# Attention with beacon keys and a gated MLP on one core: first set's first values between the second and third scores, one MLP product before the fifth

## The chip, the cores and the metric

The kernel runs on one core of a Trainium2 chip. The metric is the device time of one execution in microseconds; the time quoted for a kernel is the median of its runs. The engines are named as in the profile: PE (TensorE, matmuls), PEld (its weight loads), DVE (VectorE), ACT (ScalarE), POOL (GpSimd) and SP (SyncE, which only issues transfers here).

## The reference

Two stages follow each other, and the result of the first is the input of the second. The first is causal attention for 8 batches of 8 heads, 576 queries of 64 elements, with 16 beacon keys and values put ahead of the ordinary ones. All queries may see the beacons.

```python
k_all = np.concatenate([beacon_k, k], axis=2)
v_all = np.concatenate([beacon_v, v], axis=2)
scores = scale * np.matmul(q, k_all.transpose(0, 1, 3, 2))
scores = np.where(causal, -1000000000.0, scores)      # beacons never masked
a = np.exp(scores - scores.max(-1, keepdims=True))
a /= a.sum(-1, keepdims=True) + 1e-09
attn = np.matmul(a, v_all)
x = attn.transpose(0, 2, 1, 3).reshape(B * S, H * D)  # 4608 tokens x 512
h = x @ w_in                                          # 512 x 2048
g = h * (1.0 / (1.0 + np.exp(-1.702 * h)))
out = g @ w_out                                       # 2048 x 512
```

## The kernel before, in words

**Sets.** A set is four heads of one batch, so there are 16 sets, two to a batch. A set's scores are computed transposed: keys lie on the partitions and queries along the free axis. The first four sets ("early") are handled in two halves of 288 queries. Only the parts on or below the causal diagonal are computed. A set's scores come in chunks of at most 512 columns for each of four heads, and each chunk goes into the one PSUM tile `s` (function `e_qk`, matmuls on L434). ScalarE takes its exponential into `E` (`e_exp`, L445), which frees `s` for the next chunk. Masks then cut the diagonal blocks: on VectorE for the first half of sets 0 and 1 (`e_mask`, L459, a minimum with a constant tile), on GpSimd otherwise (L466).

**Sums and values.** `e_av` (L521) multiplies `E` with ones, which gives the sums of the softmax, and with two halves of the values `vb`; that is three products for each half of a set. Their names here are sums, first values and second values. `e_z1` (L533) transposes the sums, `e_z2` takes the reciprocal (L540) and transposes it back (L544), and `e_norm` (L556) multiplies each value product by it into `xT`, the input of the MLP.

**MLP.** Tokens go in groups: two of 256, then of 512. `e_m1` (L580) is the product with `w_in`, one PSUM tile of 512 columns at a time. For the first two groups ScalarE takes a tanh (L594) and VectorE completes the gate (L613); later groups use a GELU on ScalarE (L601). The product with `w_out` is plain for the first two groups (L625), and for the others a scheme of seven half-size products (L694) with sums before (L645) and joins after (L710) on VectorE. `xT` is a ring of four batches, and the weights arrive in pieces during the opening.

**What sets the order.** The order of the work is written out by hand, a list of numbers for each engine in `ORDER`; a number is the place of an operation in the order in which the program creates them. `Plan.run` gives each operation a planned start, from constants for durations and latencies, and emits the operations by planned start; the order on each engine is that of its list. The planned times have one more use: all products but the scores share four PSUM tiles, and `Plan.run` gives a product the tile whose last reader ends first by plan. The semaphores that really hold an engine come from the data and the tiles, not from the planned times.

**Queues.** The opening's loads of queries, keys, values and weights are issued on GpSimd, whose list also holds masks. Such a load waits for the landing of the eighth load before it. The beacon keys are issued on SP after two memsets of VectorE, and the stores leave on SP.

The numbers that the change moves are these. On TensorE: 76, 100, 106, 108 and 111 are the first to fifth scores, namely the first half of set 0, the first half of set 1, and the three chunks of the second half of set 0; 129 are the sixth, of set 1. 115, 118 and 120 are sums, first and second values of the first half of set 0; 138, 141 and 143 the same of set 1. 155 and 152 are the second and the first product of the first MLP group. On VectorE: 78 is the last mask of the first half of set 0, and 105, 104 and 102 are the masks of the first half of set 1; 87 is a memset for beacon keys. 116 and 117 are `e_z1` and `e_z2` of set 0, 119 and 121 its normalising; 139, 140, 142 and 144 are those of set 1; 157 is a gate.

The softmax here doesn't subtract the row's maximum and nothing guards it: scores larger than these inputs give would overflow.

## Time and profile before

| What | Value |
|---|---|
| Runs | 329.97, 332.07, 331.99 us |
| Median | 331.99 us |
| Span of the profiled execution | 328.1 us |
| Profiled execution's own time | not given apart from its span |
| TensorE clock granted | 1.000 over the span |
| TensorE busy | 309.3 us, 94% |
| VectorE, ScalarE, GpSimd busy | 235.9, 202.0, 114.0 us |
| First score matmul | at 8.38 us |
| TensorE's idle stretches in the opening | 2.04 us to 11.47, 2.04 us to 14.54, 1.58 us to 20.01 |
| Bytes read and written in HBM | 37.22 and 9.44 MB |

The span is the time from the first to the last instruction of one profiled execution. A line of the view in order of time reads: start in us, time from start to end of the merged instructions, engine, line of the kernel, operation, tiles written and read, their form, and how many instructions were merged; in brackets stands how long the engine was idle before it and what ended that. Matmuls are pipelined and their ends are modelled, so neighbouring lines can overlap. A line of waits reads: engine and line that waited, what it waited for, the sum in us, how often, and the longest.

### The profile page before, as it was taken

Reading aid. Unit: us, or ns where it says so; the run is one execution under the profiler, and the core shown is the slowest. Engines: PE = TensorE matmul, PEld = TensorE weight load, DVE = VectorE, ACT = ScalarE, POOL = GpSimd, SP = SyncE. Lnnn points to the kernel's source line nnn. Section 1 sums busy time; section 2 is a strip of 40 time slices with the busy share of each in tenths; the row PEclk is TensorE's granted clock in tenths of the full one; section 3 lists DMA queues with packets and bytes.
Section 4 is the critical chain, followed back from the end, with each engine's and each line's share of the span. In section 5 each row is a group of like instructions: output and inputs, shape, how many; then the busy total and the mean of one; then the engine's idle time right before and its main releaser. Section 6 shows DMA issues by size and latency. Waiting matters only on the chain.

```text
span 328.1 us, 9811 instructions
## 1 busy us (share of the span) xinstructions
PE 309.3 (94%) x4288; PEld 210.0 (64%) x4288; DVE 235.9 (72%) x478; ACT 202.0 (62%) x236; POOL 114.0 (35%) x178
## 2 busy tenths in 40 slices
PE   0489999999999999999999999999999999999995
PEld 0367665544775467745878878547764776447884
DVE  3657788777987989977998798958557843006674
ACT  1567597687767686679767686868477212674010
POOL 8765487190319312951078019400042000000000
PEclk9999999999999999999999999999999999999999
DMA  7999999194424921693029809600120012000122
GB/s 126 161 202 209 203 187 181 34 99 103 113 67 72 186 50 34 70 191 57 2 45 177 133 2 122 157 0 2 37 96 2 2 34 78 18 0 2 65 98 97
DMA packets 58219, 28.81 MB, mean 88 GB/s; under 512 B 41280, under 2 KB 53568, under 8 KB 58176
## 3 DMA queue, kind: packets, MB, share of 16 engines
q0 software_dynamic: 47552, 18.49, 47.8%
q1 hardware_dynamic: 10560, 9.69, 9.1%
q8 instruction: 33, 0.54, 0.7%
q14 instruction: 10, 0.08, 0.1%
q10 hardware_dynamic: 64, 0.01, 0.0%
HBM read 37.22 MB, written 9.44 MB: 142 GB/s over the span
## 4 chain that ended last, share of the span: by engine, by line
PE 89%; ACT 4%; DVE 3%; DMA 2%; issue 1%; POOL 0%; DVEq 0%; ACTq 0%; POOLq 0%
PE u L580 36%; PE u L694 30%; PE s L434 9%; PE u L521 9%; PE u L625 4%; ACT E L445 3%; DMA qn<-in_q_dram 2%; DVE qT L405 1%; DVE sA L645 1%; DVE xT L556 1%; DVE rz L544 0%; DVE zt L533 0%; ACT L601 0%; DVE osb L710 0%; DVE rc L540 0%
## 5 line engine op out<-in xcount | busy, mean ns | idle before, releaser
L580 PE MATMUL u<-xT,w 128*128 128x512 f16 (+1 forms) x704 | 130.4, 340 | 0.5 <-ACT g L601 0.5
L445 ACT ACTIVATE E<-s 128x2048 f16<-128x2048 f32 (+5 forms) x66 | 98.9, 1515 | 46.0 <-PE s L434 45.6
L601 ACT ACTIVATE g<-u 128x512 f16<-128x512 f32 x128 | 70.5, 598 | 53.8 <-PE u L580 53.4
L580 PEld LDWEIGHTS <-w 128*128 128x128 f16 x704 | 67.8, 98 | 53.9 <-issue 1.5
L466 POOL TENSOR_SCALAR_AFFINE_SELECT E<-E 128x512 f16<-128x512 f16 (+3 forms) x78 | 49.3, 663 | 113.4 <-ACT E L445 81.6
L710 DVE SCALAR_TENSOR_TENSOR osb<-u,osb 128x512 f32<-128x512 f32 x56 | 37.2, 682 | 24.7 <-PE u L694 22.4
L694 PEld LDWEIGHTS <-g 128*128 128x128 f16 x512 | 48.4, 98 | 9.3 <-issue 0.2
L694 PE MATMUL u<-w,g 128*128 128x256 f16 x384 | 50.6, 273 | 0.0
L434 PE MATMUL s<-qT,kT 32*128 32x32 f16 (+20 forms) x1376 | 35.4, 232 | 14.4 <-DVE qT L405 8.4
L434 PEld LDWEIGHTS <-kT 32*128 32x128 f16 x1376 | 25.8, 94 | 30.6 <-issue 15.0
L694 PEld LDWEIGHTS <-sA 128*128 128x128 f16 x384 | 36.3, 98 | 5.3 <-issue 0.3
L694 PE MATMUL u<-tB,sA 128*128 128x256 f16 x256 | 35.0, 273 | 0.1
L645 DVE TENSOR_TENSOR sA<-g 128x512 f16<-128x512 f16 x32 | 12.9, 415 | 26.2 <-ACT g L601 26.2
L556 DVE TENSOR_TENSOR xT<-u,rz 128x352 f16<-128x352 f32 (+2 forms) x52 | 25.6, 517 | 6.9 <-PE u L521 6.7
L365 POOL DMA_DIRECT2D vb<-in_v_dram x32 | 27.4, 874 | 2.3 <-DMA kn<-in_k_dram 1.5
L521 PE MATMUL u<-E,vb 128*32 128x352 f16 (+8 forms) x928 | 28.0, 267 | 0.0
L484 DVE TENSOR_TENSOR zs<-zs,E 128x1344 f16<-128x1344 f16 (+2 forms) x36 | 22.7, 633 | 5.3 <-POOL E L466 4.4
L521 PEld LDWEIGHTS <-vb 128*32 128x32 f16 (+1 forms) x928 | 20.2, 99 | 5.9 <-issue 1.7
L405 DVE STREAM_TRANSPOSE kT<-kn 128x576 f32<-128x576 f32 x16 | 20.1, 1258 | 2.4 <-DMA kn<-in_k_dram 1.6
L405 DVE STREAM_TRANSPOSE qT<-qn 128x576 f32<-128x576 f32 x16 | 19.8, 1239 | 0.1
L533 DVE STREAM_TRANSPOSE zt<-u 128x224 f32<-128x224 f32 (+2 forms) x32 | 14.9, 471 | 6.6 <-PE u L521 6.5
L484 DVE TENSOR_TENSOR zs<-E 128x1856 f16<-128x1856 f16 x12 | 15.8, 1319 | 3.3 <-POOL E L466 3.3
(44 smaller groups left out, 237.7 us busy)
## 6 DMA issues: line engine op xcount, KB each, us to landing
out_dram<-osb SPq DMA_DIRECT2D x36, 256.0 KB, 2.5
kn<-in_k_dram POOLq DMA_DIRECT2D x16, 288.0 KB, 6.7
qn<-in_q_dram POOLq DMA_DIRECT2D x16, 288.0 KB, 6.6
vb<-in_v_dram POOLq DMA_DIRECT2D x24, 128.0 KB, 6.6
w<-in_moe_w_in_dram POOLq DMA_DIRECT2D x8, 256.0 KB, 9.9
w<-in_moe_w_out_dram POOLq DMA_DIRECT2D x4, 512.0 KB, 14.2
vb<-in_v_dram POOLq DMA_DIRECT2D x8, 112.0 KB, 5.0
vb<-in_v_dram POOLq DMA_DIRECT2D x8, 80.0 KB, 7.9
```

The costliest lines, as they stand in the source:

```text
L365: nc.gpsimd.dma_start(out=t[0 : hi - lo, j, h0:h1, :], in_=v[b, h0:h1, lo:hi, :].rearrange("h n d -> n h d"),)
L405: nc.vector.transpose(out=f32(dst.rearrange("p n e -> p (n e)")).rearrange("p (r t) -> p t r", t=TR), in_=f32(src[:, :]).rearrange("p (t c ...
L434: nc.tensor.matmul(sc[:, h, o : o + w], kT[s % NB2][r : r + 32, j * P : (j + 1) * P, d], qT[s % NB2][r : r + 32, a : a + w, d], start=(d = ...
L445: nc.scalar.activation(out=Es[s][:, :, c0:c1], in_=ss[i][:, :, o : o + c1 - c0], func=AFT.Exp, scale=0.125,)
L466: nc.gpsimd.affine_select(out=blk, in_=blk, compare_op=ALU.is_ge, fill=0.0, base=off + (Nb if j == 0 else 0), pattern=[[0, Q], [1, w]], ch ...
L484: nc.vector.tensor_tensor(out=t, in0=E[:, :, Z0:S] if i == 1 else t, in1=E[:, :, wcol[i] : wcol[i] + S - a], op=ALU.add,)
L521: nc.tensor.matmul(u[32 * h : 32 * h + 32, a:e], lhs, src[0:kw, h, col : col + e - a], start=first, stop=last,)
L556: nc.vector.tensor_tensor(out=xT[:, 2 * hs + x : 2 * hs + x + n, t0 : t0 + w], in0=rings[("av", s, x, half)][:, 0 : n * w].rearrange("p (n ...
L580: nc.tensor.matmul(u[:, o + a - t0 : o + e - t0], w1t[:, kp, nt * P : (nt + 1) * P], xT[:, kp, a % XR : (e - 1) % XR + 1], start=(kp == 0) ...
L601: nc.scalar.activation(out=gts[g][:, n0:n1, 0:w], in_=rings[("m1", g, n0)][:, 0 : n * w].rearrange("p (n w) -> p n w", n=n), func=AFT.Gelu ...
L694: nc.tensor.matmul(u[:, HM * mt : HM * (mt + 1)], lhs[:, n, mt * P : (mt + 1) * P], rhs[:, n, :], start=(n == 0 and mt == 0), stop=(n == H ...
L710: nc.vector.scalar_tensor_tensor(out=osbs[(g, dst)][:, :], in0=rings[("p", g, p)][:, :], scalar=scale_of(g), in1=osbs[(g, src)][:, :], op0 ...
```

## The change

Two lists are reordered in their first rows. On TensorE the three products of the first half of set 0 come directly after the second scores; they stood, mixed with those of set 1, after the third. The products of set 1 stay after the third scores, now alone. The second product of the first MLP group comes before the fifth scores and not after them. On VectorE `e_z1` of set 0 comes before the first mask of set 1, `e_z2` of set 0 before that set's last mask, and set 0's normalising before `e_z1` of set 1. The lists of ScalarE, GpSimd, SP and the loads are the same.

The other edits concern the planner alone. Its limit of eight loads in flight is applied in the order in which loads are issued, and no longer by dependencies set at creation. The cost of a change of TensorE's mode becomes a constant, and durations change in the plan for scores, products with `E`, masks on GpSimd, sums, transposes, the weights' sums and the GELU. No instruction takes these numbers, but planned times choose the PSUM tiles.

```diff
     "PE": [
-        76, 100, 106, 138, 115, 141, 118, 143, 120, 108, 111, 155, 152, 129, 161, 158, 122, 131, 164, 167, 134, 127,
+        76, 100, 115, 118, 120, 106, 138, 141, 143, 108, 155, 111, 152, 129, 161, 158, 122, 131, 164, 167, 134, 127,
...
     "DVE": [
-        73, 74, 75, 97, 98, 99, 80, 81, 82, 78, 105, 87, 104, 102, 139, 116, 117, 121, 119, 140, 144, 142, 157, 154,
+        73, 74, 75, 97, 98, 99, 80, 81, 82, 78, 116, 105, 87, 104, 117, 102, 121, 119, 139, 140, 144, 142, 157, 154,
...
+    LANES = 8
...
+                    if o.lands is not None and len(flight) >= self.LANES:
+                        if flight[-self.LANES].end is None:
+                            break
+                        t = max(t, flight[-self.LANES].end + self.LAT["Q"])
...
-                        if o.mode != mode:
-                            dur += 95 + 0.75 * tail / 2.4
-                        mode, tail = o.mode, o.tail
+                        m = o.mode
+                        if m != mode:
+                            dur += 114
+                        mode = m
...
+                    if o.lands is not None:
+                        flight.append(o.lands)
...
-        if len(flight) >= LANES:
-            deps = list(deps) + [flight[-LANES]]
         i = plan.op("POOL", dur, deps, emit, due=due, pr=pr, name=name)
-        flight.append(plan.op("Q", ns, [i], lambda: None, name=name + "q"))
-        return flight[-1]
+        i.lands = plan.op("Q", ns, [i], lambda: None, name=name + "q")
+        return i.lands
...
-        w = sum(max(45, 2 * x / 2.4 + 6) for x in ps)
+        w = sum(2 * x / 2.4 + 10.5 for x in ps)
...
-                    d = 50 + 4 * (e - a) / 1.92 if eng == "DVE" else 140 + 0.875 * 4 * (e - a)
+                    d = 50 + 4 * (e - a) / 1.92 if eng == "DVE" else 190 + 0.9 * 4 * (e - a)
...
-                op("DVE", 75 + 0.6 * 4 * w, deps + sums[-1:], lambda i=i: e_zadd(s, i), pr=3, name="zadd")
+                op("DVE", 70 + 0.56 * 4 * w, deps + sums[-1:], lambda i=i: e_zadd(s, i), pr=3, name="zadd")
...
-                "PE", sum(y / 2.4 + 6 for y in w), deps,
+                "PE", sum(y / 2.4 + 3.2 for y in w), deps,
...
-                    "DVE", 65 + 1.045 * cols, [avs[(s, x, half)], z2s.get(two_back(s, half))], lambda h=half: e_z1(s, h), pr=0, closes=key, name="z1"
+                    "DVE", 98 + 1.045 * cols, [avs[(s, x, half)], z2s.get(two_back(s, half))], lambda h=half: e_z1(s, h), pr=0, closes=key, name="z1"
...
-                    "DVE", 310 + 1.04 * cols, [z1] + [norms.get((*two_back(s, half), y)) for y in range(2)],
+                    "DVE", 340 + 1.04 * cols, [z1] + [norms.get((*two_back(s, half), y)) for y in range(2)],
...
-            prev = [op("DVE", 1550, w2_ld + (prev if i < 3 else [tds[0]]), lambda i=i: e_t(i, "DVE"), pr=3, due=TDUE, name="t")]
+            prev = [op("DVE", 1200, w2_ld + (prev if i < 3 else [tds[0]]), lambda i=i: e_t(i, "DVE"), pr=3, due=TDUE, name="t")]
...
-                    "ACT", 480, [pe], lambda n0=n0, n1=n1: e_gelu(g, n0, n1),
+                    "ACT", 490, [pe], lambda n0=n0, n1=n1: e_gelu(g, n0, n1),
```

More of the change, by code (lines that the diff above doesn't have):

```diff
@@ L112 @@
         "eng", "dur", "deps", "pr", "due", "emit", "kind", "ring", "mode", "lat",
-        "start", "end", "left", "users", "ready", "seq", "name", "tail", "table",
+        "start", "end", "left", "users", "ready", "seq", "name", "count", "table", "lands",
     )
 class Plan:
+    LANES = 8
     LAT = {"PE": 230, "ACT": 178, "DVE": 212, "POOL": 110, "Q": 1400, "SP": 0}
@@ L127, in __init__, with op @@
         self.closers = {}
-    def op(self, eng, dur, deps, emit, kind="", pr=5, due=0, ring=None, closes=None, mode=None, name="", tail=0, table=None):
+    def op(self, eng, dur, deps, emit, kind="", pr=5, due=0, ring=None, closes=None, mode=None, name="", count=0, table=None):
         o = Op()
         o.eng, o.dur, o.emit, o.kind, o.pr, o.due = eng, dur, emit, kind, pr, due
-        o.ring, o.mode, o.name, o.tail, o.table = ring, mode, name, tail, table
+        o.ring, o.mode, o.name, o.count, o.table = ring, mode, name, count, table
         o.deps = [d for d in deps if d is not None]
-        o.start = o.end = None
+        o.start = o.end = o.lands = None
         o.users = []
@@ L150, in run @@
         free.update(POOL=900, SP=700)
-        mode, tail, table, order = "m", 0, "e", []
+        mode, table, order = "m", "e", []
         bank = [None] * self.ring
+        flight = []
         while any(todo.values()):
@@ L728, in due_of @@
         return 0 if i < NCH0 else T_ATT0 + T_CH * (i - NCH0)
-    LANES = 8
-    flight = []
     def pool_load(dur, ns, deps, emit, due=0, pr=0, name=""):
-        if len(flight) >= LANES:
-            deps = list(deps) + [flight[-LANES]]
         i = plan.op("POOL", dur, deps, emit, due=due, pr=pr, name=name)
-        flight.append(plan.op("Q", ns, [i], lambda: None, name=name + "q"))
-        return flight[-1]
+        i.lands = plan.op("Q", ns, [i], lambda: None, name=name + "q")
+        return i.lands
     op = plan.op
@@ L804, in chunk @@
         ps = [x[0] for x in qk_pieces(i)]
-        w = sum(max(45, 2 * x / 2.4 + 6) for x in ps)
+        w = sum(2 * x / 2.4 + 10.5 for x in ps)
         qks[i] = op(
             "PE", w, deps, lambda: e_qk(i), kind="qk", pr=0,
-            due=0, mode="r", name=f"qk{i}", tail=ps[-1],
+            due=0, mode="r", name=f"qk{i}",
         )
@@ L867, in values @@
             avs[(s, x, half)] = op(
-                "PE", sum(y / 2.4 + 6 for y in w), deps,
+                "PE", sum(y / 2.4 + 3.2 for y in w), deps,
                 lambda x=x, half=half: e_av(s, x, half), kind="av",
                 pr=(16 * s + (n if whole else 8 * half)) if s >= HS else half,
-                ring=key, mode="c", name=f"av{s}.{x}.{half}", tail=w[-1],
+                ring=key, mode="c", name=f"av{s}.{x}.{half}",
             )
```

## The prediction

> **What bounds the kernel now.** I read the page's busy shares first, then the chain that ended last, then the waits of TensorE after the opening, and only then the opening itself, engine by engine, in order of time. The page:

> ```profile
> PE 309.3 (94%) x4288; PEld 210.0 (64%) x4288; DVE 235.9 (72%) x478; ACT 202.0 (62%) x236; POOL 114.0 (35%) x178
> DMA  7999999194424921693029809600120012000122
> PE 89%; ACT 4%; DVE 3%; DMA 2%; issue 1%; POOL 0%; DVEq 0%; ACTq 0%; POOLq 0%
> ```

> The first line says that TensorE is busy for 94% of the 328.1 us, the third that 89% of the last chain are matmuls. The DMA digits are slices of 8.2 us: the transfers run at nine tenths or more from 8 to 57 us. The waits of TensorE from 38 us to the end are one line:

> ```profile
> PE u L580 <- ACT g L601: 0.5, 1, 0.5
> ```

> So from 38 us on there is half a microsecond of waiting to win. What is loose lies in the opening. TensorE there, columns start, length, instruction, then idle time and what ended it:

> ```profile
> 11.47 1.04 PE L434 MATMUL s<-qT,kT 32*128 32x288 f16 x24 [2.04 <-ACT E L445]
> 14.54 0.83 PE L434 MATMUL s<-qT,kT 32*128 32x288 f16 x24 [2.04 <-ACT E L445]
> 15.30 1.05 PE L521 MATMUL u<-E,ones 128*32 128x288 f16 x24
> 16.16 1.80 PE L521 MATMUL u<-E,vb 128*32 128x288 f16 x48
> 17.90 0.54 PE L434 MATMUL s<-qT,kT 32*128 32x192 f16 x24
> 20.01 0.55 PE L434 MATMUL s<-qT,kT 32*128 32x208 f16 x32 [1.58 <-ACT E L445]
> 20.49 1.92 PE L580 MATMUL u<-xT,w 128*128 128x256 f16 x16
> 22.34 0.54 PE L434 MATMUL s<-qT,kT 32*128 32x288 f16 x24
> ```

> Second scores end at 12.5; TensorE is idle for 2.04 us until ScalarE has emptied the one score tile; third scores at 14.54; then all six products of sums and values of both sets, 2.6 us (15.38 to 17.97 in the chain), and only then the fourth scores, though their exponential was done at 16.89. After them 1.58 us more of idleness. From 20.0 to 66 us TensorE has no gap over 0.14 us. VectorE in the same stretch:

> ```profile
> 13.51 0.26 DVE L459 TENSOR_TENSOR E<-E,keep 128x192 f16<-128x192 f16 x1 [1.01 <-ACT E L445]
> 13.96 0.36 DVE L459 TENSOR_TENSOR E<-E,keep 128x512 f16<-128x512 f16 x1
> 14.53 0.39 DVE L459 TENSOR_TENSOR E<-E,keepb 128x448 f16<-128x448 f16 x1 [0.21 <-ACT E L445]
> 15.98 0.91 DVE L533 STREAM_TRANSPOSE zt<-u 128x288 f32<-128x288 f32 x2 [1.06 <-PE u L521]
> 19.52 0.82 DVE L556 TENSOR_TENSOR xT<-u,rz 128x288 f16<-128x288 f32 x2
> ```

> It waits 1.01 and 1.06 us, and ends the normalising of both sets at 20.34. The third view is GpSimd, whose queue carries load issues and masks alternately:

> ```profile
> 26.43 0.75 POOL L378 DMA_DIRECT2D w<-in_moe_w_out_dram  x1 [0.53 <-DMA w<-in_moe_w_in_dram]
> 29.21 0.54 POOL L354 DMA_DIRECT2D vb<-in_beacon_v_dram  x1 [1.33 <-DMA w<-in_moe_w_out_dram]
> 29.75 1.07 POOL L466 TENSOR_SCALAR_AFFINE_SELECT E<-E 128x512 f16<-128x512 f16 x2
> ```

> The load at 29.21 is held until an earlier transfer has landed, and the last masks of the second set stand behind it.

> [...] So I checked spacing rather than 94%: the 48 matmuls of 512 columns from 70.38 take 10.52 us, 219 ns each. [...]

> **The change, part by part.** Nothing is added or removed on the chip; two engines' orders change, and constants in the planner. I follow the clock of the trace, starting from events that don't move: second scores done at 12.55, the second set's exponentials at 13.47 and 14.49.

> *Set 0's sums and values moved ahead of the third scores.* Their last mask ends at 12.49, the last value block that they need landed at 12.46. Six products took 2.6 us, so one is 0.43. Sums 12.57 to 13.00, values to 13.87: wholly inside the 2.04 us of idleness, cost nothing. If a value block came late, the product would wait at the head of the queue and the third scores with it; they have 0.67 us of cover. The third scores stay at 14.54, since ScalarE sets them.

> *Set 0's transpose of sums (z1) ahead of the second set's first mask on VectorE.* z1 began 0.17 after its product, so 13.2, and takes 0.42 to the next start. The mask that ran at 13.51 starts at 13.65, the memset of the beacon keys at 13.9 instead of 13.77 (its key loads on SP land by 21.7 and are cast at 37), the second mask at 14.1. Then reciprocal and transpose of set 0 (0.25 + 0.40) before the third mask: 15.14 to 15.53 instead of 14.53 to 14.92. This is the added cost: everything queued behind waits, and set 1's sums on TensorE start at 15.60 instead of 15.30, an idle 0.2 us.

> *What TensorE then has.* Three products of set 1, 15.60 to 16.90. The fourth scores come as their exponential ends, 16.95 instead of 17.9: **1.0 us sooner**. Set 0's two normalisings run on VectorE from 15.45 to 16.3 under set 1's products. Set 1: z1 16.2, reciprocal 16.7, transpose to 17.4, two normalisings to 18.29 (20.34 before).

> *One MLP product ahead of the fifth scores.* It needs the last normalising, so it starts at 18.36 and ends at 19.29. Its weights landed at 15.67. The fourth exponential runs 17.53 to 18.98; the fifth scores could start at 19.0 and start at 19.29: 0.3 lost there, 0.93 of MLP work done in an idle stretch of 1.58. Fifth exponential 19.93 to 21.38, second MLP product to 20.76, sixth scores 21.44. Before, they followed the second MLP product at 22.41. **Gain at this point 0.95 us.** The next product needs weights that landed at 21.39 and starts at 21.9: 0.5 of cover left. On GpSimd the first set's mask follows its exponential from 20.04 to 19.05, and the third set's key load behind it from 20.46 to 19.5; the load after that stays at 21.68, held by the landing at 21.39, and so do the masks at 22.23 to 23.30, which TensorE wants only at 23.8.

> *Where part of it goes back.* With 0.95 the second set's last exponential ends at 28.7 instead of 29.68, but its masks stand behind the load held at 29.21. That load waits for a transfer in a full DMA, which nothing here brings forward. Masks still end at 30.82. The second set's second-half sums, on TensorE at 31.46 in the chain, would be due at 30.5; they wait to 30.9 (0.05 to 0.1 after the mask, as other releases show). **0.55 us is left.** The halves after it follow with it: scores of the third set 37.24 to about 36.7, for which keys landed at 33.23 and queries at 34.20, needed at 33.9 and 35.4.

> *Later.* Fixed landings have room (kn of the fifth set 47.73 for a use at 52.05; w_out rows by 42.6 for 45.0), so 0.55 goes to the end: span 328.1 to 327.55.

> *Planner constants.* They are not instructions, but planned times choose which of four PSUM tiles a product takes. By hand, the first deals exchange tiles among themselves with each free by 0.5 us or more. Later deals I have not worked out. Gain is bounded by the 0.5 us of waits after 38 us; cost is open: each bad deal holds TensorE for up to one reader, 0.68 us for a join, 0.60 for a GELU. I take zero and keep 0.5 below, 2.5 above for the range.

> **Against the runs.** The page has no time of the profiled run but its span; 331.99 lies 3.9 above it, the lowest run 1.9. I keep 3.9: 327.55 + 3.9 = 331.4. Three runs of one kernel spread over 2.1 us, or 0.6%; one per cent (3.3 us) is about what a measurement of this kernel can tell from no change.

> **Rivals.** *The whole 0.95 arrives* (chance 0.12): the held load goes out sooner because a transfer lands sooner. For: the third set's keys are issued one microsecond earlier. Against: they are queued behind, not ahead of, what it waits for. 331.0. *Nothing is left* (0.15): VectorE's longer queue, or weights at 21.39 landing half a microsecond later, eat the rest. For: covers of 0.5; against: both stay covered in my sum. 332.0. *Slower* (0.11): the deal of PSUM tiles. Place: the eight product groups after 70 us, where ScalarE, VectorE and TensorE share four tiles. One join's wait (0.68) per group is 5.4 us less 0.55: 336.9. It decides against "no change" from 3.3 + 0.55 = 3.9 us, six such waits. Against: the same rule, earliest tile to come free, gave next to none before. *The order does nothing* (0.03): would need TensorE not to take work in the stated order; 332. *Over 1% faster* (0.04): the three idle stretches of the opening sum to 5.66 us, but 2.04 of it lies ahead of every edit; the other 3.62 would have to vanish whole, or the runs' spread help; about 328.5.

> **The numbers.** Forecast 0.55, 331.4. Within 1%: 0.55 + 0.12 + 0.15 + 0.03 = 0.85. Faster 0.04, slower 0.11. The range goes from 331.0 less the 2.0 by which a run fell below the median, 329.0, to 331.4 plus the 2.5 kept for bad deals, 333.9.

> **What would show it.** Right: sums of set 0 on TensorE at 12.6; fourth scores at 16.9; an MLP product between fourth and fifth scores from 18.4; sixth scores at 21.4; masks of set 1 still at 29.75; TensorE idle 0.3 to 0.4 before the sums behind them; third set's scores at 36.7. Wrong: values waiting for a load near 13; the third mask after 15.6; masks leaving GpSimd before 29.5; and, above all, new waits of TensorE on ScalarE or VectorE after 38 us.

## The result, and the profile after

The changed kernel takes 329.24 us, the median of eight runs between 328.77 and 329.64; the kernel before takes 330.76 next to it, eight runs between 329.97 and 332.07. The ratio is 0.9946, with a 95% interval from 0.9922 to 0.9971. So the change is worth about half a per cent, 1.5 us, where I forecast 0.55 us. Most runs of the kernel before stand at 330.3, and three to five in ten of them (16 of 54 in one set of runs, 18 of 37 in another) in a second group, most of it around 332 us; the changed kernel has no second group. That is needed below, because the median of the kernel before moves with the share of that group.

The profiled execution of the changed kernel has a span of 327.8 us, against 328.1 before. On the page, span, busy shares, transfers and chain barely move:

```profile
span 327.8 us, 9812 instructions
PE 310.9 (95%) x4288; PEld 210.6 (64%) x4288; DVE 236.4 (72%) x478; ACT 202.0 (62%) x236; POOL 114.5 (35%) x178
DMA  7999999193424921692039809600120002000122
PE 89%; ACT 4%; DVE 3%; DMA 2%; SPq 1%; issue 0%; DVEq 0%; ACTq 0%
```

TensorE is busy for 1.6 us *more* with the same 4288 matmuls: the first hint, since nothing was added. From 38 us on its waits are the same single line as before:

```profile
PE u L589 <- ACT g L610: 0.5, 1, 0.5
```

The lines of the kernel are 9 higher than before from there on (L434 is L443, L521 is L530, L580 is L589). Now the opening on TensorE, in order of time:

```profile
11.88 1.04 PE L443 MATMUL s<-qT,kT 32*128 32x288 f16 x24 [2.15 <-DVE qT L414]
12.85 0.62 PE L530 MATMUL u<-E,ones 128*32 128x288 f16 x12
13.29 1.04 PE L530 MATMUL u<-E,vb 128*32 128x288 f16 x24
14.97 0.83 PE L443 MATMUL s<-qT,kT 32*128 32x288 f16 x24 [0.65 <-ACT E L454]
15.73 0.62 PE L530 MATMUL u<-E,ones 128*32 128x288 f16 x12
16.16 1.03 PE L530 MATMUL u<-E,vb 128*32 128x288 f16 x24
17.36 0.83 PE L443 MATMUL s<-qT,kT 32*128 32x192 f16 x24 [0.16 <-ACT E L454]
18.12 1.94 PE L589 MATMUL u<-xT,w 128*128 128x256 f16 x8
20.00 0.62 PE L443 MATMUL s<-qT,kT 32*128 32x208 f16 x32
20.55 1.05 PE L589 MATMUL u<-xT,w 128*128 128x256 f16 x8
22.21 0.54 PE L443 MATMUL s<-qT,kT 32*128 32x288 f16 x24 [0.62 <-ACT E L454]
```

Two things are to be seen. The idle stretches of 2.04 and 1.58 us ahead of the third and the fifth scores have become 0.65 and nothing. And the same work has two prices: the first MLP product, 8 matmuls of 256 columns, takes 1.94 us and the second 1.05. The trace's record of the granted clock (the rate at which TensorE is let run) tells why: it begins at 20.21 us with full rate. Until then TensorE ran at half that: the last five matmuls of the first product start 213 or 214 ns apart, those of the second, from its second on, 109 or 110. So the second idle stretch went in part because the product in it took twice as long; in a second trace, e4 below, with the clock up at 18.41, 0.31 us are left of it. (The views by window print full rate for a stretch that lies ahead of the first record; there the spacing of the matmuls is the evidence.) In the trace of the kernel before, the rise stood at 17.73 us, ahead of its MLP products. On VectorE:

```profile
13.52 0.48 DVE L542 STREAM_TRANSPOSE zt<-u 128x288 f32<-128x288 f32 x1 [0.73 <-PE u L530]
13.93 0.26 DVE L468 TENSOR_TENSOR E<-E,keep 128x192 f16<-128x192 f16 x1
15.30 0.35 DVE L468 TENSOR_TENSOR E<-E,keepb 128x448 f16<-128x448 f16 x1
17.75 0.82 DVE L565 TENSOR_TENSOR xT<-u,rz 128x288 f16<-128x288 f32 x2
```

The last line ends at 18.57, where it ended at 20.34 before, though this execution's third scores began 0.43 us later: its queries landed later.

What I passed over shows in the traces below. They hold half-rate stretches of 3.41 us (e9, from 21.52), 6.83 (e8, 13.43 to 20.26) and 10.24 (e5, 13.57 to 23.81), which are one, two and three times 3.41, and the rise lies at another place in each of seven traces of the kernel before, between 17.68 and 19.18 us.

### The profile page after: what moved, and what is told of

Same layout as the page of the kernel before. It is cut to its first block, busy times and chain, and to the rows that moved or that the text cites. A ratio compares the mean times of both kernels' runs of the same rounds, so it can differ in the third digit from the quotient of the medians.

```text
span 327.8 us, 9812 instructions
## 1 busy us (share of the span) xinstructions
PE 310.9 (95%) x4288; PEld 210.6 (64%) x4288; DVE 236.4 (72%) x478; ACT 202.0 (62%) x236; POOL 114.5 (35%) x178
## 4 chain that ended last, share of the span: by engine, by line
PE 89%; ACT 4%; DVE 3%; DMA 2%; SPq 1%; issue 0%; DVEq 0%; ACTq 0%
PE u L589 37%; PE u L703 30%; PE u L530 9%; PE s L443 9%; PE u L634 5%; ACT E L454 3%; DMA bkf<-in_beacon_k_dram 2%; DVE sA L654 1%; SPq L393 1%; ACT L610 0%; DVE kT L414 0%; DVE qT L414 0%; DVE rz L553 0%; DVE xT L565 0%; DVE zt L542 0%
## 5 line engine op out<-in xcount | busy, mean ns | idle before, releaser
L589 PE MATMUL u<-xT,w 128*128 128x512 f16 (+1 forms) x704 | 131.5, 342 | 0.5 <-ACT g L610 0.5
L589 PEld LDWEIGHTS <-w 128*128 128x128 f16 x704 | 68.0, 98 | 54.3 <-issue 1.7
L719 DVE SCALAR_TENSOR_TENSOR osb<-u,osb 128x512 f32<-128x512 f32 x56 | 37.2, 683 | 24.5 <-PE u L703 22.5
L443 PE MATMUL s<-qT,kT 32*128 32x32 f16 (+20 forms) x1376 | 35.8, 234 | 12.5 <-DVE qT L414 10.8
L443 PEld LDWEIGHTS <-kT 32*128 32x128 f16 x1376 | 26.1, 95 | 29.4 <-issue 13.6
L530 PE MATMUL u<-E,vb 128*32 128x352 f16 (+8 forms) x928 | 28.2, 268 | 0.0
L530 PEld LDWEIGHTS <-vb 128*32 128x32 f16 (+1 forms) x928 | 20.2, 98 | 5.9 <-issue 1.7
```

The source lines that it names most:

```text
L443: nc.tensor.matmul(sc[:, h, o : o + w], kT[s % NB2][r : r + 32, j * P : (j + 1) * P, d], qT[s % NB2][r : r + 32, a : a + w, d], start=(d = ...
L530: nc.tensor.matmul(u[32 * h : 32 * h + 32, a:e], lhs, src[0:kw, h, col : col + e - a], start=first, stop=last,)
L589: nc.tensor.matmul(u[:, o + a - t0 : o + e - t0], w1t[:, kp, nt * P : (nt + 1) * P], xT[:, kp, a % XR : (e - 1) % XR + 1], start=(kp == 0) ...
L719: nc.vector.scalar_tensor_tensor(out=osbs[(g, dst)][:, :], in0=rings[("p", g, p)][:, :], scalar=scale_of(g), in1=osbs[(g, src)][:, :], op0 ...
```

## The experiments

Two theories stood against each other at first. **A:** the order is worth what its waits give, and on top of it TensorE's half clock in the opening costs the two orders different amounts. **B:** the clock rises where the program puts it and has no part in the gain. A third, **C**, was the rival of the prediction: the planner's constants and the deal of PSUM tiles.

To compare traces in spite of different landings of the first loads, I use the time from the start of the third scores, which ScalarE sets in both orders, to the end of the span. In the table, "rise" is the last time in the opening at which the clock goes to full.

| Trace | Rise, us | Third to sixth scores | Third scores to end |
|---|---|---|---|
| before | 17.73 | 7.80 | 313.54 |
| before, six more traces | 17.68 to 19.18 | 7.60 to 8.17 | 313.35 to 313.93 |
| after | 20.21 | 7.24 | 312.85 |
| after again (e4) | 18.41 | 6.92 | 312.52 |
| order only (e2) | 21.41 | 7.42 | 313.02 |
| sets only (e11) | 24.42 | 9.07 | 314.81 |
| MLP product only (e12) | 24.96 | 9.20 | 315.28 |

### The kernel before and the changed kernel once more; order and constants apart

e1 and e4 are the two kernels unchanged. e2 takes the two lists of the change and leaves the planner as it was; e3 the reverse.

```diff
 e2, against before: only the first rows of "PE" and "DVE" in ORDER
-        76, 100, 106, 138, 115, 141, 118, 143, 120, 108, 111, 155, 152,
+        76, 100, 115, 118, 120, 106, 138, 141, 143, 108, 155, 111, 152,
-        78, 105, 87, 104, 102, 139, 116, 117, 121, 119, 140, 144, 142,
+        78, 116, 105, 87, 104, 117, 102, 121, 119, 139, 140, 144, 142,
 e3, against after: the same four lines the other way round
```

> The kernel before, unchanged, once more: what the comparison itself can tell, and a second trace of the same program. Theory A (clock): the time at which TensorE's granted clock rises to full (17.73 us in the trace of before, 20.21 us in that of after) differs from run to run of one kernel, and is what spreads the runs of before over 2 us; this trace should show another time for the rise, and products of 512 columns in the opening at about 430 ns instead of 218 until then. Theory B (order alone): the rise is where the program's work puts it, so it is again at 17.7 us within 0.3. Ratio 1.000 within its interval either way, single runs between 329.9 and 332.1.

> The two reordered lists of the change with the planner constants of the kernel before. If the order makes the gain (A and B alike): 329.2, the same as the changed kernel, ratio 0.9946 within 0.002. Theory C (deal of PSUM tiles by the new constants): 330.3, half of the gain or less.

> The planner constants of the change with the two lists of the kernel before. A and B: no change, ratio 1.000 within 0.002, about 330.8. C: the constants bring 0.5 us or more, 330.2 or less.

> The changed kernel, unchanged, once more. A: the rise of the clock again at another time than 20.21 us, and single runs spread by less than those of before, 328.8 to 329.7, since less of TensorE's work is bunched behind the opening. B: rise at 20.2 within 0.3. Both: ratio 0.9946 within 0.002, masks of the second set again behind the load held until 29.2 us.

| Kernel | Median, us | Runs | Ratio to before, 95% |
|---|---|---|---|
| e1 before again | 330.55 | 329.53 to 333.95 | 1.0000 [0.9977, 1.0023] |
| e2 order only | 329.21 | 328.69 to 330.12 | 0.9951 [0.9933, 0.9970] |
| e3 constants only | 330.64 | 330.16 to 333.31 | 1.0005 [0.9979, 1.0031] |
| e4 after again | 329.25 | 328.95 to 329.75 | 0.9951 [0.9933, 0.9970] |

The order makes the whole gain, and the constants alone make none that shows (e3's interval reaches from 0.9979 to 1.0031): theory C falls, with the second group of runs present in e1 and e3 and absent in e2 and e4. The rise moved from 20.21 to 18.41 in the changed kernel unchanged. In e1 it stands at 17.93, within the 0.3 us that B allowed; over all traces of the kernel before it lies between 17.68 and 19.18. So B's fixed rise falls. What the rise does to the changed kernel is little: from 18.41 to 21.41 the time behind the third scores grows by 0.5 us, in three traces.

### The two halves of the change apart

e11 leaves the MLP product where it was; e12 moves only that product, with the planner constants of the change.

```diff
 e11, against after
-        76, 100, 115, 118, 120, 106, 138, 141, 143, 108, 155, 111, 152,
+        76, 100, 115, 118, 120, 106, 138, 141, 143, 108, 111, 155, 152,
 e12, against after (the VectorE list is that of before)
-        76, 100, 115, 118, 120, 106, 138, 141, 143, 108, 155, 111, 152,
+        76, 100, 106, 138, 115, 141, 118, 143, 120, 108, 155, 111, 152,
```

> The changed kernel without the move of the MLP product: its second product of the first group comes after the fifth scores again. By my steps the set moves bring the fourth scores 1.0 us forward; the fifth scores start at 19.4 in that trace's time, the two MLP products follow and end at 21.4 under full clock, so that this is 0 to 0.2 us slower than the change at full clock and 0.3 to 0.8 slower under half clock. 329.5.

> The kernel before with the MLP product before the fifth scores and the planner constants of the change, without the moves of set 0. The product waits for the last normalising at 20.3 us, where the fifth scores started at 20.0, so they, their exponential and the sixth scores come 1.3 us later, with 0.9 us of TensorE work in exchange: 0.3 to 0.8 us slower than before, 331.1. If the single move alone brings the gain: 329.5.

e11: 331.11 us, ratio 0.9991 [0.9972, 1.0009]. e12: 331.17 us, 1.0013 [0.9994, 1.0032]. Neither half can be told from no change, and together they give 0.9946. I had expected e12 at 331.1, which came true, and e11 at 329.5; that is a miss of 1.6 us, and its trace shows how it comes:

```profile
17.30 0.83 PE L443 MATMUL s<-qT,kT 32*128 32x192 f16 x24 [0.16 <-ACT E L454]
19.69 0.83 PE L443 MATMUL s<-qT,kT 32*128 32x208 f16 x32 [1.56 <-ACT E L454]
20.45 3.59 PE L589 MATMUL u<-xT,w 128*128 128x256 f16 x16
23.98 0.72 PE L443 MATMUL s<-qT,kT 32*128 32x288 f16 x24
```

The fourth scores are early, as in the full change, but the idle stretch of 1.56 us behind them is back. The 16 matmuls of the two MLP products then run at half rate, 3.59 us instead of 1.92 in the kernel before, and the clock rises only at 24.42. The microsecond won is gone by the sixth scores. The fastest of its runs took 329.35, as the changed kernel does.

### A clock that is up before the first scores

To take the half clock away I gave TensorE work that nobody reads, in the 8 us in which it waits for its first inputs.

```diff
+    warm = cst.tile([P, 512], F16, tag="warm", name="warm")
+    nc.vector.memset(warm, 0.0)
+    wu = psu.tile([P, 512], F32, tag="u3", name="u3")
+    for _ in range(17):
+        nc.tensor.matmul(wu[:, :], warm[:, 0:P], warm[:, :], start=True, stop=True)
```

> The kernel before with 17 products of a zeroed tile (128x128 by 512 columns, into a PSUM tile that nothing reads) on TensorE ahead of the first scores, while it waits for its inputs until 8.4 us; nothing else is changed or left out. Theory A (the rise of the clock varies from run to run, 17.7, 17.9 and 18.9 us in three traces with the list of before, and a late rise leaves TensorE at half rate in its continuous stretch from 20 us): with the clock up ahead of the first scores, all runs lie close together, none above 331, and the median is 329.2, since the second set's masks behind the held load still end at 30.8 us. Theory B (spread has another source): runs between 331.5 and 334 remain, about 3 in 10.

> The same 17 products ahead of the changed kernel. A: the opening gets faster (fourth scores before 16.5 us, first MLP product 0.9 instead of 1.3 to 1.9 us long), but TensorE then waits for the masks of the second set, which end at 30.8, and the end moves by 0.3 us or less: 329.0, and before and after differ by 0.2 us at most once both are warm. Rival (the order is worth its microsecond under either clock): 1 us less than the warmed kernel before.

e5: 330.25 us, 0.9983 [0.9964, 1.0001], with 7 of 22 runs above 331.3. e6: 329.23 us, 0.9937 [0.9914, 0.9960]. The forecast for e5 failed: the second group stayed. So did A's forecast for e6, a difference of 0.2 us at most between the two: it is 1.0, as the rival had it. The traces say why. In e5's profiled execution, which took 331.57 us, the unread products started 427 ns apart and from the rise on 216 ns; the clock rose at 6.74 and fell again. In the view by stretch, the busy times of PE, PEld, DVE, ACT and POOL stand behind the length, and the granted clock is the third number from the end:

```profile
6.80:13.50 6.70, 2.42 (x54) 1.46 (x53) 4.88 (x10) 2.91 (x4) 6.05 (x10) 1.00 1.59 160
13.60:23.80 10.20, 7.71 (x165) 6.00 (x165) 4.93 (x14) 5.22 (x4) 6.04 (x11) 0.50 1.40 195
23.90:30.00 6.10, 6.10 (x138) 4.82 (x137) 3.77 (x8) 5.60 (x8) 3.12 (x6) 1.00 1.25 208
```

Behind an idle stretch of 3.03 us up to the second scores, TensorE runs at half rate from 13.57 to 23.81, and the first two MLP products lie in it:

```profile
21.12 3.21 PE L586 MATMUL u<-xT,w 128*128 128x256 f16 x16
24.27 0.54 PE L440 MATMUL s<-qT,kT 32*128 32x288 f16 x24
```

They take 3.21 us where the kernel before took 1.92, and the sixth scores come 9.75 us behind the third instead of 7.8. Here, moreover, the mean granted clock of each run tells how long it was at half rate after its first rise, the end of the kernel included. Of the 22 runs of e5 those at 0.990 (6.8 us at half rate) took 329.98 to 330.50, with one at 331.53; those at 0.984 (10.2 us) took 331.32 to 332.02; the one at 0.979 took 332.33. Two at 0.994 and 0.995 took 329.49 and 329.79; one at 0.987, with 329.50, does not fit. But for it and the one at 331.53, the time goes in steps with stretches of 3.41 us.

Next I tried to keep the clock up with more such products between the scores.

```diff
 e9, against before with the 17 products; e10 and e13 with {0: 8}
+        for _ in range({0: 8, 1: 5}.get(i, 0)):      # at the end of the scores of chunk i
+            nc.tensor.matmul(wu[:, :], warm[:, 0:P], warm[:, :], start=True, stop=True)
```

> The kernel before with the 17 products ahead of the first scores and, so that TensorE does not go idle and its clock does not fall again as it did in the warmed kernels (full rate from 6.74 to 13.57 us, half until 23.81 in the slow one), 8 more behind the first scores and 5 behind the second, all into the tile that nothing reads. Theory A (time under half clock behind 16 us sets both the level and the spread of before): no runs above 330.6 any more, the upper group of 3 in 10 gone, median 329.3 or less. If the upper group stays while the trace shows full clock through 14 to 24 us, A falls.

> The changed kernel with the 17 products and 8 behind the first scores. A: clock full through the opening, fourth scores at 16.6, sixth scores at 21.0, then TensorE waits for the masks behind the held load; 328.7, the fastest runs of the warmed kernel. Against the filled kernel before: 0.3 to 0.7 us faster, so that less than half of the change's 1.3 us is the order under a full clock, and the rest is what the order saves when the clock is late.

e10 does what it was made for: full clock from 6.05 to 326.9 in its trace (two of its eight runs have a mean of 0.995), 329.12 us, 0.9943 [0.9919, 0.9968]. But it is no faster than the changed kernel at 329.24, where I had expected 0.5 us. e9 went the other way: 332.07 us, 1.0034 [1.0017, 1.0051], slower than the kernel before. Its clock was full from 4.45 to 21.52, and its scores came early; then it fell just where the dense work begins:

```profile
16.69 0.54 PE L440 MATMUL s<-qT,kT 32*128 32x192 f16 x24
18.80 0.50 PE L440 MATMUL s<-qT,kT 32*128 32x208 f16 x24 [1.58 <-ACT E L453]
21.16 0.23 PE L440 MATMUL s<-qT,kT 32*128 32x32 f16 x8 [1.86 <-issue]
21.32 3.44 PE L588 MATMUL u<-xT,w 128*128 128x256 f16 x16
```

```profile
21.60:24.90 3.30, 3.30 (x20) 2.02 (x21) 0.00 (x0) 1.39 (x2) 2.29 (x5) 0.50 1.24 205
```

Between 17.2 and 21.2 us TensorE is idle for 3.44 us in two stretches, and the clock goes down behind them. One run of e9 kept full clock throughout (mean 1.0) and took 329.93; those at 0.992 to 0.995 took 331.44 to 332.36, those at 0.988 and 0.989 332.49 to 333.57. So the answer to e9's own question is that its filler did not keep the clock up where it counts, and that the kernel before is slow when it is down there. The 1.86 us of "issue" inside the fifth scores I can't explain; no other trace has it, so part of what made e9's profiled execution slow may be peculiar to it.

With the same 17 products ahead (e5 and e6) the changed order is faster by 1.0 us in the median (330.25 to 329.23), and by 0.8 in the fastest run of each (329.49 to 328.67), though neither kept its clock up. Under full clock there is one run to go by: e9's 329.93, against a median of 329.12 for the six runs of e10 with a mean of 0.999 or 1.000. That is 0.8 us for the order there, as far as one run can tell, where I had expected 0.3 to 0.7.

### Where the rest of the gain would go: the held load

e7 takes the two masks of the second set out from behind the load of beacon values that is held to 29.2 us; e8 does so with the 17 products, e13 with the fillers too.

```diff
     "POOL": [
-        59, 133, 61, 136, 137, 63,
+        59, 133, 136, 137, 61, 63,
```

> The changed kernel with the last two masks of the second set ahead of the held load of beacon values on GpSimd (136, 137, 61 instead of 61, 136, 137). My prediction's step (0.4 us of the gain goes back behind the held load): 0.3 to 0.4 us faster than the changed kernel, 328.9. The traces of the changed kernel, where TensorE reaches the sums at 31.04 and 31.27 without a wait and the masks end at 30.84 and 30.82: no difference, 329.2, because the half clock has already eaten it.

> Both: 17 products ahead and the two masks ahead of the held load, on the changed kernel. If half clock and held load are the two things that take the gain one after the other, only this one gets it: sums of the second set's second half on TensorE at about 30.0 us instead of 31.3, third set's scores at 35.8, median 328.4. If either alone is all there is: no better than the one of the other two that is faster.

> The filled changed kernel (17 products ahead, 8 behind the first scores, clock full from 6 us on in its trace) with the two masks of the second set ahead of the held load. There TensorE reached the second set's second-half sums at 30.23 us and had to wait inside them to 31.1. If the held load is what takes the gain once the clock is full: sums without a wait at 30.2, third set's scores at 35.5 to 36.0, median 328.3. If something else is next (weights, the third set's keys at 33.2): 329.0, as the filled kernel.

e7: 329.05 us, 0.9934 [0.9914, 0.9955]. e8: 329.49, 0.9946 [0.9926, 0.9967]. e13: 329.00, 0.9939 [0.9916, 0.9962]. None can be told from the changed kernel, and e8 and e13 missed their forecasts by 1.1 and 0.7 us; e7's median lies between its two answers. e8 was no test of a full clock: in its trace it was down from 13.43 to 20.26. The traces show that the load does hold something, but only where the clock is up early. e10 has it:

```profile
29.42 0.54 POOL L369 DMA_DIRECT2D vb<-in_beacon_v_dram  x1 [1.36 <-DMA w<-in_moe_w_out_dram]
29.96 1.07 POOL L483 TENSOR_SCALAR_AFFINE_SELECT E<-E 128x512 f16<-128x512 f16 x2
```

```profile
30.23 1.06 PE L538 MATMUL u<-E,ones 128*32 128x288 f16 x20
31.11 1.76 PE L538 MATMUL u<-E,vb 128*32 128x288 f16 x60
```

The sums are reached at 30.23 and drag until the masks end at 31.03. With the masks first (e13) they run from 29.99 without a wait:

```profile
28.34 1.06 POOL L483 TENSOR_SCALAR_AFFINE_SELECT E<-E 128x512 f16<-128x512 f16 x2 [0.65 <-ACT E L462]
29.35 0.54 POOL L369 DMA_DIRECT2D vb<-in_beacon_v_dram  x1
```

The third set's scores then come at 35.82 instead of 36.38. Counted from the third scores that is 0.37 us, and at the end 0.15 are left, too little for the medians to show. In the changed kernel as it is, the step does not arise: TensorE reached the sums at 31.27 and, in e4, 31.04, behind masks that ended at 30.82 and 30.84.

### The second group of runs

Five more traces of the kernel before were meant to catch a run around 332 us.

> A look at the kernel before, for a trace of its upper group (331.5 to 333.9 us, 3 runs in 10). Theory A: in such a run the clock rises behind 20 us, at 21 to 25, and the first two MLP products take 2.6 to 3.6 us together instead of 1.9; in a run of the lower group it rises before 19. Rival: the upper group has the same rise and loses its time elsewhere, behind 40 us.

> The same look once more, as one in three is expected to fall into the upper group: rise behind 20 us if above 331.3, before 19 us if below.

> The same look once more: rise behind 20 us if above 331.3, before 19 us if below.

> A fourth look at the kernel before. The five traces of its order of the opening so far lie between 330.0 and 330.7 us with the rise at 17.7 to 18.7. If this one is above 331.3: rise behind 20 us, first two MLP products together above 2.6 us. If below: rise before 19.

> A fifth look, with the same two answers: above 331.3 us with a rise behind 20 us, or below with a rise before 19 us.

They took 330.70, 329.96, 330.35, 330.49 and 330.35, with the rise at 18.67, 17.68, 18.60, 19.18 and 18.61. None fell into the second group. Four rose before 19 us, as I had expected of the lower group, and e17 at 19.18. A late rise goes with a slow run in the traces of four kernels made from the same opening (e5, e9, e11, e12: last rises at 23.81 to 24.96, runs of 331.43 to 332.05 us). In the unmodified kernel itself no trace shows it.

The clock records of all twenty traces lead further, though I worked this out only after the runs. In each, the changes of the clock stand whole multiples of 3.413 us apart, to the fall at the end of the kernel (before: 310.61 us behind the rise, 91 times that; after: 307.20, 90 times). So each trace can be cut at its own changes into stretches of 3.413 us. At half rate, the clock rose behind each of the 25 stretches in which TensorE was busy for 2.78 us or more, and behind none of the 63 with 2.77 or less. In the trace of before the last three stretches ahead of the rise hold 1.04, 1.04 and 3.19 us of work, in that of after 1.50, 2.77 and 3.25. The closest on either side are from e15 (rise at 17.68) and the changed kernel (no rise until 20.21), and the third line is e11's, with the idle stretch of 1.56 us in it and no rise until 24.42:

```profile
14.27:17.68 3.41, 2.78 (x80) 2.22 (x83) 2.08 (x7) 2.03 (x2) 1.55 (x3) 1.00 1.72 182
13.38:16.80 3.42, 2.77 (x86) 2.05 (x77) 3.22 (x10) 2.48 (x3) 2.04 (x4) 1.00 1.68 176
17.59:21.00 3.41, 1.85 (x59) 1.57 (x49) 0.82 (x2) 1.87 (x2) 2.29 (x4) 1.00 1.26 199
```

Where the stretches lie differs from run to run (rises at 17.68 to 19.18 us in the seven traces of the kernel before). My estimate takes every position for equally likely and lays them over the opening of the kernel before in e17, which ran at half rate to 19.18 us. The first stretch with 2.78 us of work then ends at 17.6 to 19.8 us for 62% of the positions, at 23.5 to 24.5 for 29% and at 26.6 to 26.9 for 8%; e3's opening gives the same shares. (With a limit of 2.70 or 2.85 us in place of 2.78 they are 67, 29 and 4% or 58, 29 and 13%.)

Of the 176 runs of the kernel before whose clock is recorded in the sets next to e1 to e13 and in e1, 107 (61%) took less than 331.1 us, 55 (31%) 331.4 to 332.6 and 14 (8%) 332.9 to 334.0. The opening of the changed order in e2 has no such gap: all positions end up with a rise at 18.1 to 21.5. The mean clocks fit too: a rise at 26.6 to 26.9 puts the fall at the end, 89 stretches later as in e11 and e12, at 330.4 to 330.7 us, inside a span of 331.2 to 332.2, and all 14 of the slowest runs have a mean of 0.998 or 0.999, while the 55 have 1.000. By this estimate, then, the second group comes from the idle stretch ahead of the fifth scores, which costs some runs the rise ahead of their dense work. This is worked out and not seen: the limit was found in the same traces, TensorE's busy times are modelled at their ends, and a trace of the group is missing.

## Why the prediction was right and wrong

**Right, with its sizes.** TensorE bounds the kernel, the opening is where something is loose, and nothing moved behind 38 us. Set 0's products fit into the idle stretch: sums 0.97 behind the start of the second scores, forecast 1.1. No value block was late: the last landed at 13.09 and the values started at 13.29, which is 0.2 us of cover where I had counted 0.5. The fourth scores start 2.39 us behind the third instead of 3.36: 0.97 sooner, forecast 1.0. The second set's last mask ends at 15.65, 0.68 us behind the start of the third scores; I had forecast 0.99 behind it, and the 0.2 us of idleness that I had counted ahead of that set's sums did not come in this trace (0.18 us did in e10). The third set's keys, issued sooner, did not land sooner: they were issued at 19.25 us in e9 and at 21.34 in e14, and landed at 32.98 and 32.92. The masks behind the held load stayed at 29.75. The planner's constants did nothing that shows (e3), which disposes of the rival that would have ended slower.

**Wrong, the half clock (the step "one MLP product ahead of the fifth scores").** I gave the moved product 0.93 us and the fourth and fifth scores half a microsecond each, rates from rows behind 17.73 us, where that trace has full clock. They took 1.94 or 1.32, and 0.83 and 0.62 or 0.55: the clock had not risen yet. I had looked at the granted clock's mean, 1.000, and not at where its record began. So the gain at the sixth scores, forecast 0.95, measured 0.56 in the trace after, 0.38 in e2, and 0.88 in e4, where the clock rose at 18.41. A small correction the other way: two of the product's eight matmuls need only set 0's columns and start 0.9 us before the rest in e10 (17.30 and 18.25).

**Wrong, the give-back (the step "where part of it goes back").** I let 0.4 us of the gain be lost behind the held load. At the clock that the changed kernel really has, TensorE arrives too late to be held (31.27 us, the masks end at 30.82). At the end the traces with the changed order (three, rises 18.41 to 21.41) stand at 312.5 to 313.0 behind the third scores, the seven of the kernel before at 313.35 to 313.93: means 312.80 and 313.63, a gain of **0.83** where I forecast 0.55. The two errors had opposite signs and nearly cancelled in the pair of traces before and after (313.54 to 312.85, 0.69 us): that this is near 0.55 is luck.

**Wrong, what else the order is worth (the step "against the runs").** This is the larger part of the miss, and it is not in the pair of traces. I took the spread of 2.1 us over three runs for noise of the measurement, put it into the range alone and gave the change no part in it. The runs show it to be a property of the kernel before: its lower group stands at 330.3 to 330.4 and the changed kernel at 329.2, which is 1.1 us, and the second group adds 0.2 to 0.5 to the difference of medians. In the changed kernel that group is absent: 39 runs of the two kernels with its order (e2 and both sets of runs of the changed kernel) all lie below 330.2. Of the 1.5 us measured, then, about 0.4 is the second group. The 1.1 us and the 0.83 of the traces leave 0.3 open; the three traces of the order are of runs of 329.29 to 329.91 us, slower than its median. Why the order spares the changed kernel a second group is worked out above from the stretches of the clock and not shown by a trace of the group.

**Wrong, the base.** I added 3.9 us around the span, from a median of three of which two belong to the second group. The profiled execution of e1 has 1.7 around its span (328.4 and 330.10), so the trace of the kernel before belonged to a run of about 329.8 (or 329.97, if it was the lowest of the three). With 329.8 as its base the sum would have read 329.25; that 329.24 was measured would then have been luck, since the gain in it, 0.55, is too small and that run of the kernel before faster than most. The forecast of 331.4 was high by that term. The gain itself, 0.55 us or 0.17%, was a third of the 0.54% measured. The range from 329.0 held the time only by its lower edge.

**What else was not in the sum.** The forecast also leaned on one trace at a favourable clock: with the rise at 17.73 it is among the earliest of the seven.

## What to carry to other kernels

Before a stage's durations are priced from rows of the same trace, look up where the granted clock's record begins and what the same matmul costs on both sides of it (in the trace after, eight matmuls of 256 columns took 1.94 us ahead of 20.21 and 1.05 behind it); the mean of 1.000 over the span before said nothing of the 17.73 us ahead of its first record. In e11 an idle stretch of 1.56 us on TensorE went with a loss greater than its length: the clock was still down in the dense work behind it, which took 3.59 us instead of 1.92, and from the third scores to the end it took 1.96 us more than the changed kernel. So two moves that gained nothing each, e11 and e12 (0.9991 and 1.0013), gained together (0.9946), since only both closed the gap. And where a kernel's runs stand in two groups, that is a finding to be explained, and the base of a sum should be the group that the profiled run belongs to.
